# Seven half-block products for eight in the last batch's spatial gate of a fused attention and gated-MLP kernel

## Chip, cores and metric

The kernel runs on one core of a Trainium2 chip. Its time is the device time in microseconds of one execution; a number given for a kernel is the median of several runs. The profile is one further execution, taken by the hardware profiler, with a time of its own.

## What is computed

Four batches, 1088 positions, 128 model columns (4 heads of 32). Attention comes first, with a kernel feature map of 64 features, then a gated MLP with a spatial gate. The reference, cut to what matters:

```python
x = attn_out.transpose(0, 2, 1, 3).reshape(B, S, H * D)    # [4, 1088, 128]
h = gelu_tanh(x @ w_in)                                    # [4, 1088, 1024]
u, v = h[..., :512], h[..., 512:]
v_n = (v - mean(v)) / sqrt(var(v) + 1e-6) * g_ln           # over the 512 columns
v_s = einsum('ts,bsd->btd', w_sg, v_n) + b_sg[None, :, None]
out = x + (u * v_s) @ w_out
```

The change is in the einsum with `w_sg`, a 1088 x 1088 matrix, for the last batch. That product is most of TensorE's work.

## The kernel before

**Words.** TensorE multiplies in float32r. For accuracy each float32 operand is split in two words, a high one (the value cast to float32r) and a low one (the value less the high word), and three products are summed: high x high, high x low, low x high. A "word h" is a cast on ScalarE or in a transfer on POOL's queue, a "word l" a subtraction on VectorE.

**The spatial product.** The sum over s is cut in nine row blocks t of 128 (the last is half full: both words stand on its two halves, so it takes two matmuls for three). The output is [128 columns d, rows of W]: four d-blocks `db`, and the 1088 rows in three thirds `ci` of 362, 362 and 364. A unit (db, ci) takes one PSUM bank and 8 x 3 + 2 = 26 matmuls: `z_hi` with both words of V (`parts`) on `w_h[t]`, `z_lo` with V's high word on `w_l[t]`. W's words stay in SBUF for the whole run: `w_h`, one tile of nine row blocks, written by casting transfers, and `w_l`, eight tiles, subtracted in batch 0 (`w_lo`).

**Around it.** `v1` makes v = x @ w_in for a row block, `gelu` takes it out of PSUM, `bn` takes its statistics, `norm` works out the scale and shift for the first five and then for the last four row blocks, on VectorE, and `v3` applies them on ScalarE. `vh` and `vl` split V. `pu` and `ug` make u for a unit. After a unit `gt` (`scale`) takes z out of PSUM with `g_col` and the bias on VectorE, `gm` (`gate`) multiplies with u, `gh` and `gl` split the result, and `po` adds its product with w_out to an accumulator that is open over the four d-blocks. `o1`, `o2` add x, `st` stores. The very last unit (3, 2) of batch 3 is done in two halves with an unsplit product (`last`). Attention of a batch (`k1` to `xl`) runs beside the spatial product of the batch before it; POOL makes its low words `ql`.

**What sets the order.** Every step is registered with `at(name, function)`, and `Steps.run` issues them by `WHEN`, a list written out with one place for each step. Each engine and each queue then runs its own instructions in that order. Steps are named here as they are in the code, `z 3 0 1 4` for `("z", 3, 0, 1, 4)`: batch, d-block, third, row block. SP's queue takes the plain transfers, POOL's the casting ones. Buffers come from one pool by tag; a tile waits until the last reader of the buffer's tile before has finished. PSUM has eight banks, all under one tag.

In the order before, batch 3 takes the units one after the other. Lines of the profile: L840 and L849 are `z_hi` and `z_lo`, L864 to L866 `unit`, L910 to L913 `out`, L877 `scale`, L884 `gate`, L889 and L892 `g_h` and `g_l`, L827 and L832 `split_h` and `split_l`, L708 `w_lo`, L749 `gelu`, L289 the casting load of W, L514 `ql`, L917 to L926 the last unit.

Of the kernel before, what the change touches and what calls it, by code (L numbers as in the profile page):

```python
# [1123 lines left out]
```

## Time and profile before

| | us |
|---|---|
| Median of 3 runs (327.08 to 327.32) | 327.14 |
| The profiled execution, its own time | 327.86 |
| Its span, from the first to the last instruction | 325.8 |
| TensorE busy | 318.4 (98%), 2282 matmuls |
| VectorE busy | 251.6 (77%) |
| ScalarE busy | 158.8 (49%) |
| POOL busy | 22.8 (7%) |

Matmuls are pipelined: a record lasts 0.32 us though the next one starts after half of that, so that a busy TensorE isn't one at its peak. An engine's waits, and the distance from one start to the next, say more. The granted clock is given as a share of 2.4 GHz.

### The profile page before, as it was taken

Reading aid. Unit: us, or ns where it says so; the run is one execution under the profiler, and the core shown is the slowest. Engines: PE = TensorE matmul, PEld = TensorE weight load, DVE = VectorE, ACT = ScalarE, POOL = GpSimd, SP = SyncE. Lnnn points to the kernel's source line nnn. Section 1 sums busy time; section 2 is a strip of 40 time slices with the busy share of each in tenths; the row PEclk is TensorE's granted clock in tenths of the full one; section 3 lists DMA queues with packets and bytes.
Section 4 is the critical chain, followed back from the end, with each engine's and each line's share of the span. In section 5 each row is a group of like instructions: output and inputs, shape, how many; then the busy total and the mean of one; then the engine's idle time right before and its main releaser. Section 6 shows DMA issues by size and latency. Waiting matters only on the chain.

```text
span 325.8 us, 5961 instructions
## 1 busy us (share of the span) xinstructions
PE 318.4 (98%) x2282; PEld 304.7 (93%) x2282; DVE 251.6 (77%) x614; ACT 158.8 (49%) x347; POOL 22.8 (7%) x35
## 2 busy tenths in 40 slices
PE   7999999999999999999999999999999999999995
PEld 5777999899999999999999999999999999999993
DVE  5899999999998967597988967768998874443243
ACT  4579714646549734354629815244634954131210
POOL 0300000022200000202200000112200000000000
PEclk9999999999999999999999999999999999999999
DMA  7999934774000115832000012551000000000002
GB/s 218 370 423 348 404 137 131 175 180 118 2 0 0 48 49 138 194 96 57 2 0 24 2 68 47 109 94 45 2 1 2 24 35 11 0 2 0 0 2 68
DMA packets 14091, 29.55 MB, mean 91 GB/s; under 512 B 1744, under 2 KB 10224, under 8 KB 13680
## 3 DMA queue, kind: packets, MB, share of 16 engines
q1 hardware_dynamic: 13344, 23.87, 25.1%
q0 software_dynamic: 720, 5.31, 4.3%
q8 instruction: 18, 0.29, 0.4%
q14 instruction: 9, 0.07, 0.1%
HBM read 23.19 MB, written 2.65 MB: 79 GB/s over the span
## 4 chain that ended last, share of the span: by engine, by line
PE 82%; DVE 11%; ACT 3%; DMA 2%; issue 1%; SPq 1%; ACTq 0%; DVEq 0%
PE pz L840 38%; PE pz L849 17%; PE pu L864 3%; DVE w_l L708 2%; PE po L913 2%; PE pu L866 2%; PE po L911 2%; PE pu L865 2%; PE po L910 2%; PE pkv L420 2%; PE pv L736 2%; PE pv L735 2%; PE pv L744 2%; DMA vn<-in_q 2%; PE pk L388 1%
## 5 line engine op out<-in xcount | busy, mean ns | idle before, releaser
L840 PE MATMUL pz<-w_h,vl 128*128 128x362 f32 (+1 forms) x432 | 140.1, 325 | 0.4 <-DVE vl L832 0.4
L840 PE MATMUL pz<-w_h,vh 128*128 128x362 f32 (+1 forms) x432 | 140.1, 325 | 0.0
L849 PE MATMUL pz<-w_l,vh 128*128 128x362 f32 (+1 forms) x384 | 118.0, 324 | 0.0
L840 PEld LDWEIGHTS pz<-w_h,vl 128*128 128x128 f32 x432 | 81.1, 188 | 1.4 <-DVE vl L832 0.9
L840 PEld LDWEIGHTS pz<-w_h,vh 128*128 128x128 f32 x432 | 81.1, 188 | 1.0 <-ACT u L871 0.3
L849 PEld LDWEIGHTS pz<-w_l,vh 128*128 128x128 f32 x384 | 71.1, 188 | 0.1
L877 DVE SCALAR_TENSOR_TENSOR gt<-pz,vi,b_bc 128x362 f32<-128x362 f32 (+3 forms) x49 | 28.5, 584 | 38.6 <-PE pz L840 38.3
L889 ACT CAST gh<-gt 128x362 fp32r<-128x362 f32 (+1 forms) x47 | 23.0, 493 | 53.6 <-DVE gt L884 49.8
L871 ACT ACTIVATE u<-pu 128x362 f32<-128x362 f32 (+1 forms) x48 | 22.7, 472 | 24.6 <-PE pu L866 16.2
L892 DVE TENSOR_TENSOR gl<-gt,gh 128x362 fp32r<-128x362 f32 (+1 forms) x47 | 26.4, 563 | 9.8 <-ACT gh L889 9.7
L827 ACT CAST vh<-vn 128x128 fp32r<-128x128 f32 (+1 forms) x72 | 25.8, 403 | 13.8 <-PE pz L840 13.4
L832 DVE TENSOR_TENSOR vl<-vn,vh 128x128 fp32r<-128x128 f32 (+1 forms) x72 | 28.5, 419 | 2.0 <-ACT vh L827 1.8
L817 ACT ACTIVATE vn<-vn,nm,rs 128x512 f32<-128x512 f32 x36 | 28.2, 811 | 2.6 <-DVE nm L811 2.5
L884 DVE TENSOR_TENSOR gt<-gt,u 128x362 f32<-128x362 f32 (+3 forms) x49 | 25.9, 528 | 0.9
L749 ACT ACTIVATE vn<-pv 128x512 f32<-128x512 f32 x36 | 21.0, 597 | 8.6 <-PE pv L744 7.7
L765 DVE BATCH_NORM_STATS2 st<-vn 128x6 f32<-128x512 f32 x33 | 22.5, 683 | 2.9 <-ACT vn L749 2.4
L535 DVE RECIPROCAL den<-den 128x362 f32<-128x362 f32 (+1 forms) x9 | 21.8, 2417 | 2.9 <-ACT den L530 2.9
L514 POOL TENSOR_TENSOR qpl<-e_0a,qph 128x362 fp32r<-128x362 f32 x6 | 6.5, 1103 | 145.2 <-ACT qph L509 145.2
L864 PE MATMUL pu<-x_h,win_h 128*128 128x362 f32 (+1 forms) x48 | 16.2, 338 | 0.0
L866 PE MATMUL pu<-x_l,win_h 128*128 128x362 f32 (+1 forms) x48 | 15.7, 327 | 0.0
L865 PE MATMUL pu<-x_h,win_l 128*128 128x362 f32 (+1 forms) x48 | 15.6, 326 | 0.0
L913 PE MATMUL po<-gl,wout_h 128*128 128x362 f32 (+1 forms) x47 | 15.5, 329 | 0.0
(181 smaller groups left out, 429.1 us busy)
## 6 DMA issues: line engine op xcount, KB each, us to landing
w_f<-in_w SPq DMA_DIRECT2D x9, 576.0 KB
w_h<-in_w POOLq DMA_DIRECT2D x2, 1152.0 KB, 8.9
vi<-in_v SPq DMA_DIRECT2D x7, 288.0 KB
w_h<-in_w POOLq DMA_DIRECT2D x1, 1728.0 KB, 15.7
k<-in_k SPq DMA_DIRECT2D x3, 576.0 KB
out<-o SPq DMA_DIRECT2D x8, 181.0 KB
w_h<-in_w POOLq DMA_DIRECT2D x2, 576.0 KB, 8.3
e_2a<-ab SPq DMA_DIRECT2D x6, 182.0 KB
```

Source lines behind the costliest of these rows:

```text
L765: V.bn_stats(st, self.vn[:, t])
L817: A.activation(self.vn[:, t], self.vn[:, t], AF.Identity, bias=self.nm[:, t : t + 1], scale=self.rs[:, t : t + 1])
L827: A.copy(self.parts[db][0][:, ts], self.vn[:, ts, P * db : P * db + P])
L832: V.tensor_sub(vl[:, ts], self.vn[:, ts, P * db : P * db + P], f32(vh[:, ts]))
L840: mm(self.z[db, ci], lhsT=self.parts[db][i][:, t], rhs=T["w_h"][:, t, AT[ci] : AT[ci] + cw], start=(t == 0 and i == 0), stop=(t == NT - 1 ...
L849: mm(self.z[db, ci], lhsT=self.parts[db][0][:, t], rhs=T["w_l", t][:, AT[ci] : AT[ci] + CH[ci][1]], start=False, stop=False,)
L864: mm(pu, lhsT=T["win_h"][:, ws], rhs=xh[:, cs], start=True, stop=False)
L871: A.activation(self.u[db, ci], self.pu.pop((db, ci)), AF.Gelu_apprx_tanh)
L877: V.scalar_tensor_tensor(self.gt[db, ci][:, s], self.z[db, ci][:, s], T["g_col"][:, db : db + 1], T["b_bc"][:, c0 : c0 + cw][:, s], op0=AL ...
L884: V.tensor_mul(gt, gt, self.u[db, ci][:, s])
L889: A.copy(self.g[db, ci][0], self.gt[db, ci])
L892: V.tensor_sub(self.g[db, ci][1], self.gt.pop((db, ci)), f32(self.g[db, ci][0]))
```

## The change

In batch 3 only, for the first two thirds of the rows (`ci` 0 and 1, 362 each) and the row blocks 0 to 7, the spatial product is taken as a 2 x 2 block product. The d-blocks go in two pairs, (0, 2) and (1, 3). With A the V blocks (two d-blocks x two halves of four row blocks) and B the W blocks (two halves x two thirds), the four results need eight products A x B of 4 row blocks; the new code takes seven, in four accumulators `x`, `w`, `u` and `v`, with sums of blocks as operands:

- sums of V (`s1` to `s4`), on VectorE, written over halves of `vn` that are no longer read;
- sums of W (`t1` to `t4`), by a copy and an accumulating transfer each in DRAM, in batches 0 to 2, on POOL's queue; in batch 3 they are loaded into SBUF once plain (`ldT`, into one buffer under `kld`; `ldT1`, into `vx` and one tile) and once cast (`Th`, `Th1`), and VectorE makes the low words (`Tl`, `Tl1`). `t1` goes over W's blocks of the second third, the others into buffers that attention has finished with;
- results by `take`: a product that belongs to several results is taken out of PSUM by VectorE several times, into running sums (`acc`, in `vx`) with plus or minus `g_col`, and the last time into `gt`.

The ninth row block is added with its own words (`edge`, `rest`). The last third keeps its 26 matmuls (`third`), with the new words' tiles. Each `product` has 4 x 3 matmuls. From step `z 2 0 1 4` on, the whole order `WHEN` is new: in batch 2, too, units of several d-blocks are interleaved, and attention of batch 3, the loads of the sums and the matmuls that don't need them stand in other places. Ahead of that only the eight transfers in DRAM and one small multiplication are put in. The pads, some tile sizes, and the tag of one small tile (`wout_f`) change as well.

```diff
+PAIRS = ((0, 2), (1, 3))
...
+    class Fast(Gate):
...
+        def sums(self, j, n):
+            d1, d2 = PAIRS[j]
+            a11, a12, a21, a22 = (self.half(d, k) for d in (d1, d2) for k in range(2))
+            o, x, y = {
+                "s1": (a22, a21, a22), "s3": (a21, a21, a11), "s2": (a22, a11, a22), "s4": (a12, a12, a22),
+            }[n]
+            V.tensor_sub(o, x, y)
...
+        def product(self, j, o, left, right, t, first):
+            p = self.open((j, o))[:, : CH[0][1]]
+            w = self.words[j, left]
+            h, l = self.right(right, t)
+            mm(p, lhsT=w[:, 0, t], rhs=h, start=first, stop=False, **GO)
+            mm(p, lhsT=w[:, 0, t], rhs=l, start=False, stop=False, **GO)
+            mm(p, lhsT=w[:, 1, t], rhs=h, start=False, stop=t == 3, **GO)
...
+        def take(self, j, o, db, ci, first, final, g):
+            c0, cw = CH[ci]
+            z, add = self.open((j, o))[:, :cw], T["b_bc"][:, c0 : c0 + cw]
+            if not first:
+                add = self.acc[db, ci]
...
+            V.scalar_tensor_tensor(to, z, T[g][:, db : db + 1], add, op0=ALU.mult, op1=ALU.add)
...
+    class Sums:
...
+        PARTS = (
+            ("t2", 2, 1, "s", 0), ("t2", 3, 1, "s", 1), ("t3", 2, 1, "q", 2), ("t2", 0, 2, "e", 3),
+            ("t3", 3, 1, "ab", 5), ("t3", 0, 2, "e", 6), ("t4", 0, 1, "r", 8), ("t4", 1, 3, "x", 9),
+        )
...
+        def copy(self, n):
+            self.d[n] = dram.tile([P, 4, WP], F32, tag=n, name=f"w{n}", bufs=1)
+            of = {"t1": (0, 0), "t3": (0, 1)}
+            nc.gpsimd.dma_start(self.d[n], self.block(*of[n]) if n in of else self.d["t1" if n == "t2" else "t2"])
+
+        def add(self, n):
+            of = {"t1": (0, 1), "t2": (1, 1), "t3": (1, 1), "t4": (1, 0)}[n]
+            nc.gpsimd.dma_start(self.d[n], self.block(*of), accum_op=ALU.add)
...
+        def load(self, i):
+            n, t, k, tag, at = self.PARTS[i]
+            if at // 3 not in self.raw:
+                self.raw[at // 3] = new([P, 3, WP], "kld", f"wr{at // 3}")
+            load(self.of(i), self.d[n][:, t : t + k])
...
+        def high(self, i):
+            n, t, k, tag, at = self.PARTS[i]
+            self.w[i] = h, l = [new([P, k, WP], tag, f"w{n}_{t}{x}", F32R) for x in "hl"]
...
+            nc.gpsimd.dma_start(h, self.d[n][:, t : t + k])
+
+        def low(self, i):
+            h, l = self.w[i]
+            V.tensor_sub(l[:, :, : CH[0][1]], self.of(i)[:, :, : CH[0][1]], f32(h[:, :, : CH[0][1]]))
...
+            third(d1)
+            products("x", a11, (0, 0), True)
...
+            for db, ci in ((d1, 1), (d2, 0), (d2, 1)):
+                taken("x", db, ci, first=True, g_col="ng_col" if ci else "g_col")
+            products("x", a12, (1, 0), False)
+            rest("x", d1, 0)
...
+            taken("x", d1, 0, first=True, final=True)
...
+            products("w", "s1", "t1", True)
+            taken("w", d2, 1)
+            products("w", "s4", (1, 1), False)
+            rest("w", d1, 1)
+            taken("w", d1, 1)
...
+            products("u", "s2", "t2", True)
...
+            taken("u", d1, 1, final=True)
...
+            products("u", "s3", "t3", False)
+            taken("u", d2, 0, g_col="ng_col")
+            rest("u", d2, 1)
...
+            taken("u", d2, 1, final=True)
+            products("v", a22, "t4", True)
+            rest("v", d2, 0)
...
+            taken("v", d2, 0, final=True)
...
-        g = Gate(b)
+        g = (Fast if b == B - 1 else Gate)(b)
```

## Rows read from the trace of the kernel before

**Rows 1.** The page, busy time: us, share of the span, instructions.

```profile
PE 318.4 (98%) x2282; PEld 304.7 (93%) x2282; DVE 251.6 (77%) x614; ACT 158.8 (49%) x347; POOL 22.8 (7%) x35
```

**Rows 2.** Waits of PE, whole run: us in total, times, longest.

```profile
PE pn L597 <- DMA vn<-in_q: 1.3, 2, 0.9
...
PE pz L840 <- DVE vl L832: 0.4, 1, 0.4
```

**Rows 3.** Stretches: length, busy us of PE, PEld, DVE, ACT, POOL; clock, DMA share, GB/s.

```profile
80.00:110.00 30.00, 30.00 (x176) 28.83 (x175) 28.17 (x78) 20.93 (x44) 2.16 (x3) 1.00 0.04 13
230.00:260.00 30.00, 30.00 (x178) 29.07 (x177) 27.25 (x73) 17.15 (x35) 0.98 (x1) 1.00 0.02 8
190.00:230.00 40.00, 40.00 (x330) 39.14 (x329) 28.19 (x59) 15.94 (x35) 5.13 (x5) 1.00 0.33 70
260.00:319.20 59.20, 59.20 (x368) 59.20 (x367) 25.53 (x51) 16.71 (x39) 0.00 (x0) 1.00 0.02 7
```

**Rows 4.** Timeline of PE: start, us; first and last matmul of unit (1, 1), batch 3.

```profile
279.50 0.32 PE L840 MATMUL pz<-w_h,vh 128*128 128x362 f32 x1
...
283.50 0.32 PE L840 MATMUL pz<-w_h,vl 128*128 128x362 f32 x1
```

**Rows 5.** Groups by line and form, 195 to 326 us (the last: 20 to 50).

```profile
L877 DVE SCALAR_TENSOR_TENSOR gt<-pz,vi,b_bc 128x362 f32<-128x362 f32 x14 | 8.3, 594 | 16.1 <-PE pz L840 16.0
L892 DVE TENSOR_TENSOR gl<-gt,gh 128x362 fp32r<-128x362 f32 x14 | 8.1, 581 | 5.4 <-ACT gh L889 5.4
L832 DVE TENSOR_TENSOR vl<-vn,vh 128x384 fp32r<-128x384 f32 x15 | 7.6, 550 | 0.0
L884 DVE TENSOR_TENSOR gt<-gt,u 128x362 f32<-128x362 f32 x14 | 7.5, 535 | 0.4
...
L827 ACT CAST vh<-vn 128x384 fp32r<-128x384 f32 x15 | 6.8, 510 | 9.0 <-PE pz L840 9.0
...
L749 ACT ACTIVATE vn<-pv 128x512 f32<-128x512 f32 x9 | 5.4, 597 | 3.6 <-PE pv L744 3.2
...
L832 DVE TENSOR_TENSOR vl<-vn,vh 128x128 fp32r<-128x128 f32 x9 | 2.5, 288 | 0.9 <-ACT vh L827 0.9
...
L827 ACT CAST vh<-vn 128x128 fp32r<-128x128 f32 x9 | 2.4, 293 | 0.1
...
L708 DVE TENSOR_TENSOR w_l<-w_f,w_h 128x1104 fp32r<-128x1104 f32 x8 | 10.4, 1301 | 0.0
```

**Rows 6.** Timeline of DVE, back to back: start, us.

```profile
264.79 0.54 DVE L884 TENSOR_TENSOR gt<-gt,u 128x362 f32<-128x362 f32 x1
265.24 1.02 DVE L832 TENSOR_TENSOR vl<-vn,vh 128x384 fp32r<-128x384 f32 x2
```

**Rows 7.** Waits of DVE, 190 to 326 us: in total, times, longest.

```profile
DVE gt L877 <- PE pz L840: 32.6, 17, 3.8
...
DVE gl L892 <- ACT gh L889: 8.0, 14, 0.7
```

**Rows 8.** POOL: issues (mean ns); landings in the page (KB, us); three operations.

```profile
L289 POOL DMA_DIRECT2D w_h<-in_w x5 | 2.8, 583 | 0.0
...
w_h<-in_w POOLq DMA_DIRECT2D x2, 1152.0 KB, 8.9
...
w_h<-in_w POOLq DMA_DIRECT2D x1, 1728.0 KB, 15.7
...
86.29 1.91 POOL L514 TENSOR_TENSOR qpl<-e_2a,qph 128x364 fp32r<-128x364 f32 x2 [7.10 <-ACT qph L509]
...
212.81 1.24 POOL L514 TENSOR_TENSOR qpl<-e_0a,qph 128x362 fp32r<-128x362 f32 x1 [1.50 <-ACT qph L509]
220.61 0.97 POOL L514 TENSOR_TENSOR qpl<-e_1a,qph 128x362 fp32r<-128x362 f32 x1 [6.55 <-ACT qph L509]
```

**Rows 9.** The chain that ended last, in order of time, after the last `z`.

```profile
319.18 0.03 issue
...
322.07 0.27 DVE o L926
```

More of the change, by code (lines that the diff above doesn't have):

```diff
@@ L31 @@
 SUMS = (0,1,2)
+PAIRS = ((0, 2), (1, 3))
+GO = dict(skip_group_check=True)
 WARM = 14
@@ L280, in w_f @@
     def w_f(t):
+        if "pad_w" not in T:
+            const("pad_w", [P, 40])
         if ("w_f", t) not in T:
@@ L291, in gate_wh @@
     def gate_wh():
-        G.tensor_copy(new([P, 40], "wait", "wait", I32)[:, :1], T["vi"].bitcast(I32)[:, :1])
+        G.tensor_copy(new([P, 64], "wait", "wait", I32)[:, :1], T["vi"].bitcast(I32)[:, :1])
     def gate_wf():
@@ L447, in load_q @@
             c0, cw = CH[ci]
-            self.q[ci] = q = new([P, CW], "q", f"q{self.b}_{ci}")
+            self.q[ci] = q = new([P, WP], "q", f"q{self.b}_{ci}")
             load(q[:, :cw], qd[self.b, :, c0 : c0 + cw])
@@ L610, in qa @@
     def qa(c, p):
-        if "pad_r" not in T:
-            const("pad_r", [P, 32])
         a_s[c, p] = new([P, WP], "r", f"a0_{c}{p}")[:, :n0]
@@ L895, in prepare @@
             if i == 0:
-                self.wf = new([P, C], "kld", "wout_f")
+                self.wf = new([P, C], "kp", "wout_f")
                 V.tensor_add(self.wf, f32(T["wout_h"][:, NB - 1]), f32(T["wout_l"][:, NB - 1]))
@@ L934, in store, with __init__, half, block @@
             load(outd[self.b, :, c0 : c0 + cw][:, s], self.o[ci][:, s])
+    class Fast(Gate):
+        SLOT = dict(s1="vh", s2="vh", s3="vl", s4="vl")
+        def __init__(self, b):
+            super().__init__(b)
+            self.words, self.acc, self.bank, self.n = {}, {}, {}, {}
+        def half(self, db, k):
+            return self.vn[:, 4 * k : 4 * k + 4, P * db : P * db + P]
+        def block(self, j, n):
+            if (j, n) not in self.words:
+                tag = self.SLOT[n] if n in self.SLOT else "vl" if n[1] else "vh"
+                self.words[j, n] = new([P, 2, NT // 2, P], tag, f"wb{self.b}_{j}{n if n in self.SLOT else n[0] + 4 * n[1]}", F32R)
+            return self.words[j, n]
+        def edge(self, db):
+            if db not in self.words:
+                self.words[db] = new([P, 2, P], "kb", f"we{self.b}_{db}", F32R)
+            return self.words[db]
+        def source(self, j, n):
+            d1, d2 = PAIRS[j]
+            return self.half(*{"s1": (d2, 1), "s2": (d2, 1), "s3": (d2, 0), "s4": (d1, 1)}.get(n, n))
+        def word_h(self, j, n, t0, k):
+            A.copy(self.block(j, n)[:, 0, t0 : t0 + k], self.source(j, n)[:, t0 : t0 + k])
+        def word_l(self, j, n, t0, k):
+            w = self.block(j, n)
+            V.tensor_sub(w[:, 1, t0 : t0 + k], self.source(j, n)[:, t0 : t0 + k], f32(w[:, 0, t0 : t0 + k]))
+        def edge_h(self, db):
+            A.copy(self.edge(db)[:, 0], self.vn[:, NT - 1, P * db : P * db + P])
+        def edge_l(self, db):
+            w = self.edge(db)
+            V.tensor_sub(w[:, 1], self.vn[:, NT - 1, P * db : P * db + P], f32(w[:, 0]))
+        def sums(self, j, n):
+            d1, d2 = PAIRS[j]
+            a11, a12, a21, a22 = (self.half(d, k) for d in (d1, d2) for k in range(2))
[3 more added lines that the diff above has]
+            V.tensor_sub(o, x, y)
+        def right(self, n, t):
+            if n[0] == "t":
+                return T[n, t]
+            k, ci = n
+            cs = slice(AT[ci], AT[ci] + CH[ci][1])
+            return T["w_h"][:, 4 * k + t, cs], T["w_l", 4 * k + t][:, cs]
+        def open(self, o):
+            if o not in self.bank:
+                self.bank[o] = bank(f"pz{self.b}_{o}")
+            return self.bank[o]
+        def product(self, j, o, left, right, t, first):
[5 more added lines that the diff above has]
+            mm(p, lhsT=w[:, 1, t], rhs=h, start=False, stop=t == 3, **GO)
+        def rest(self, j, o, db, ci):
+            p = self.open((j, o))[:, : CH[0][1]]
+            for i in range(2):
+                mm(
+                    p, lhsT=self.words[db][:, i], rhs=T["w_h"][:, NT - 1, AT[ci] : AT[ci] + CH[ci][1]],
+                    start=False, stop=i == 1, **GO,
+                )
[4 more added lines that the diff above has]
+                add = self.acc[db, ci]
+            if final:
+                to = self.gt[db, ci] = new([P, CW], "gt", f"gt{self.b}_{db}_{ci}")[:, :cw]
+            elif first:
+                i = db // 2 if ci else 2
+                to = self.acc[db, ci] = T["vx"].rearrange("p n c -> p (n c)")[:, WP * i : WP * i + cw]
+            else:
+                to = add
+            V.scalar_tensor_tensor(to, z, T[g][:, db : db + 1], add, op0=ALU.mult, op1=ALU.add)
+        def third(self, db, t):
+            j, m = db % 2, db // 2
+            ci = len(CH) - 1
+            cs = slice(AT[ci], AT[ci] + CH[ci][1])
+            if t == 0:
+                self.z[db, ci] = bank(f"pz{self.b}_{db}_{ci}")[:, : CH[ci][1]]
+            if t == NT - 1:
+                for i in range(2):
+                    mm(self.z[db, ci], lhsT=self.words[db][:, i], rhs=T["w_h"][:, t, cs], start=False, stop=i == 1)
+                return
+            w = self.words[j, (db, t // 4)]
+            for q, (i, r) in enumerate(((0, T["w_h"][:, t]), (0, T["w_l", t]), (1, T["w_h"][:, t]))):
+                mm(self.z[db, ci], lhsT=w[:, i, t % 4], rhs=r[:, cs], start=(t == 0 and q == 0), stop=False)
+        def out(self, db, ci):
+            cw = CH[ci][1]
+            k = self.n[ci, "o"] = self.n.get((ci, "o"), 0) + 1
+            if k == 1:
+                self.po[ci] = bank(f"po{self.b}_{ci}")[:, :cw]
+            o = self.po[ci]
+            gh, gl = self.g.pop((db, ci))
+            mm(o, lhsT=T["wout_h"][:, db], rhs=gh, start=(k == 1), stop=False)
+            mm(o, lhsT=T["wout_l"][:, db], rhs=gh, start=False, stop=False)
+            mm(o, lhsT=T["wout_h"][:, db], rhs=gl, start=False, stop=k == NB - (ci == len(CH) - 1))
@@ new lines, in tile_kernel, with __init__, block, of @@
+    class Sums:
+        PARTS = (
+            ("t2", 2, 1, "s", 0), ("t2", 3, 1, "s", 1), ("t3", 2, 1, "q", 2), ("t2", 0, 2, "e", 3),
+            ("t3", 3, 1, "ab", 5), ("t3", 0, 2, "e", 6), ("t4", 0, 1, "r", 8), ("t4", 1, 3, "x", 9),
+        )
+        def __init__(self):
+            self.d, self.raw, self.w = {}, {}, {}
+        def block(self, k, ci):
+            return wd[:, 4 * k : 4 * k + 4, AT[ci] : AT[ci] + WP]
+        def copy(self, n):
[5 more added lines that the diff above has]
+            nc.gpsimd.dma_start(self.d[n], self.block(*of), accum_op=ALU.add)
+        def of(self, i):
+            n, t, k, tag, at = self.PARTS[i]
+            return self.raw[at // 3][:, at % 3 : at % 3 + k]
+        def load(self, i):
[4 more added lines that the diff above has]
+        def high(self, i):
+            n, t, k, tag, at = self.PARTS[i]
+            self.w[i] = h, l = [new([P, k, WP], tag, f"w{n}_{t}{x}", F32R) for x in "hl"]
+            for m in range(k):
+                T[n, t + m] = h[:, m, : CH[0][1]], l[:, m, : CH[0][1]]
+            nc.gpsimd.dma_start(h, self.d[n][:, t : t + k])
+        def low(self, i):
+            h, l = self.w[i]
+            V.tensor_sub(l[:, :, : CH[0][1]], self.of(i)[:, :, : CH[0][1]], f32(h[:, :, : CH[0][1]]))
+        def first(self, t):
+            v = T["vx"].rearrange("p n c -> p (n c)")[:, : 3 * WP].rearrange("p (n c) -> p n c", c=WP)
+            return v[:, t] if t < 3 else self.last
+        def load1(self, i):
+            if i:
+                self.last = new([P, WP], "wa", "wa")
+                load(self.last, self.d["t1"][:, 3])
+            else:
+                v = T["vx"].rearrange("p n c -> p (n c)")[:, : 3 * WP].rearrange("p (n c) -> p n c", c=WP)
+                load(v, self.d["t1"][:, :3])
+        def high1(self):
+            cs = slice(AT[1], AT[1] + CH[1][1])
+            for t in range(4):
+                T["t1", t] = T["w_h"][:, t, cs], T["w_l", t][:, cs]
+            nc.gpsimd.dma_start(T["w_h"][:, :4, cs], self.d["t1"][:, :, : CH[1][1]])
+        def low1(self, t):
+            h, l = T["t1", t]
+            V.tensor_sub(l, self.first(t)[:, : CH[1][1]], f32(h))
@@ L950, in gated @@
             return last(g, db, ci)
-        at(("gt", g.b, db, ci), lambda: g.scale(db, ci))
+        if not (isinstance(g, Fast) and ci < 2):
+            at(("gt", g.b, db, ci), lambda: g.scale(db, ci))
         at(("gm", g.b, db, ci), lambda: g.gate(db, ci))
@@ L1027, in main, with fast, pair, words @@
                 gated(g, db, ci)
+    def fast(g):
+        w = Sums()
+        at("ng", lambda: V.tensor_scalar_mul(const("ng_col", [P, NB]), T["g_col"], -1.0))
+        for n in ("t1", "t2", "t3", "t4"):
+            at(("wd", n), lambda n=n: w.copy(n))
+            at(("wd", n, 1), lambda n=n: w.add(n))
+        for i in range(len(w.PARTS)):
+            at(("ldT", i), lambda i=i: w.load(i))
+            at(("Th", i), lambda i=i: w.high(i))
+            at(("Tl", i), lambda i=i: w.low(i))
+        for i in range(2):
+            at(("ldT1", i), lambda i=i: w.load1(i))
+        at("Th1", w.high1)
+        for t in range(4):
+            at(("Tl1", t), lambda t=t: w.low1(t))
+        def pair(j, d1, d2):
+            def words(n, step):
+                for t in range(0, 4, step):
+                    at(("vh", g.b, j, n, t), lambda t=t: g.word_h(j, n, t, step))
+                    at(("vl", g.b, j, n, t), lambda t=t: g.word_l(j, n, t, step))
+            def products(o, left, right, first):
+                for t in range(4):
+                    at(("p", g.b, j, o, left, t), lambda t=t: g.product(j, o, left, right, t, first and t == 0))
+            def taken(o, db, ci, first=False, final=False, g_col="g_col"):
+                if final:
+                    at(("gt", g.b, db, ci), lambda: g.take(j, o, db, ci, first, True, g_col))
+                    gated(g, db, ci)
+                else:
+                    at(("tk", g.b, j, o, db, ci), lambda: g.take(j, o, db, ci, first, False, g_col))
+            def rest(o, db, ci):
+                at(("p8", g.b, j, o, db, ci), lambda: g.rest(j, o, db, ci))
+            def third(db):
+                unit(g, db, 2)
+                for t in range(NT):
+                    at(("z", g.b, db, 2, t), lambda t=t: g.third(db, t))
+                gated(g, db, 2)
+            a11, a12, a21, a22 = ((d, k) for d in (d1, d2) for k in range(2))
+            for n in (a11, a12):
+                words(n, 4 if j else 1)
+            at(("vh", g.b, j, 8, d1), lambda: g.edge_h(d1))
+            at(("vl", g.b, j, 8, d1), lambda: g.edge_l(d1))
+            third(d1)
+            products("x", a11, (0, 0), True)
+            for n in (a21, a22):
+                words(n, 4)
+            at(("vh", g.b, j, 8, d2), lambda: g.edge_h(d2))
+            at(("vl", g.b, j, 8, d2), lambda: g.edge_l(d2))
+            for db, ci in ((d1, 1), (d2, 0), (d2, 1)):
+                taken("x", db, ci, first=True, g_col="ng_col" if ci else "g_col")
+            products("x", a12, (1, 0), False)
+            rest("x", d1, 0)
+            unit(g, d1, 0)
+            taken("x", d1, 0, first=True, final=True)
+            if not j:
+                third(d2)
+            at(("s", g.b, j, "s1"), lambda: g.sums(j, "s1"))
+            words("s1", 4)
+            for n in ("s3", "s2", "s4"):
+                at(("s", g.b, j, n), lambda n=n: g.sums(j, n))
+            words("s4", 4)
+            products("w", "s1", "t1", True)
[3 more added lines that the diff above has]
+            taken("w", d1, 1)
+            words("s2", 4)
+            products("u", "s2", "t2", True)
+            unit(g, d1, 1)
+            taken("u", d1, 1, final=True)
+            words("s3", 4)
+            products("u", "s3", "t3", False)
+            taken("u", d2, 0, g_col="ng_col")
+            rest("u", d2, 1)
+            unit(g, d2, 1)
+            taken("u", d2, 1, final=True)
+            products("v", a22, "t4", True)
+            rest("v", d2, 0)
+            unit(g, d2, 0)
+            taken("v", d2, 0, final=True)
+            if j:
+                third(d2)
+        for j, (d1, d2) in enumerate(PAIRS):
+            pair(j, d1, d2)
@@ L1077, in tile_kernel @@
                 at(("prep", i), lambda i=i, g=g: g.prepare(i))
-        main(g, 0)
+        if b == B - 1:
+            fast(g)
+        else:
+            main(g, 0)
     steps.run(tc)
```

5 lines of the change are left out of this document (4 added, 1 removed), and 130 rows, old and new, of the table WHEN.

## The prediction

> **What bounds the kernel now.** I read the page's busy shares first, then the engine's waits, then the stretches, then single instructions. TensorE is busy 98% of the span [rows 1]; that alone doesn't make it the bound, since matmuls overlap in the records. The waits settle it: over the whole run PE's longest wait is 1.3 us, for a load at the start, and the one on VectorE's word `vl` is 0.4 us [rows 2]. Between 80 and 319 us there is no stretch in which PE is below its full length [rows 3]. So a matmul less in batch 3 shortens the run by the time from one matmul's start to the next, as long as nothing makes PE wait. That time isn't the recorded 0.32 us: in unit (1, 1) of batch 3 the first matmul starts at 279.50 and the 26th at 283.50, 25 steps in 4.00 us, 0.160 us each for 362 columns [rows 4]. The granted clock is 1.00 in every stretch [rows 3], the 2.4 GHz level.
>
> **What it removes.** For each pair of d-blocks, (0, 2) and (1, 3), and the first two thirds of the rows, eight half products of 4 x 3 matmuls become seven. The ninth row block (`rest`) and the last third (`third`) keep their counts: 84 + 4 x 2 + 2 x 26 = 144 matmuls a pair for 6 x 26 = 156. Two pairs save 24, all of 362 columns: 24 x 0.160 = **3.85 us** off PE [rows 4]. The Trainium skill ("TensorE: Matmul & The Clock Gate", section "Back-to-back issue gap") gives N/2.4 + 2.5 ns for a lone warm matmul, 153 ns for 362 columns; by it the same 24 would be worth an estimated 3.7 us.
>
> **What it adds to VectorE.** Durations are from [rows 5]. A 512-column word or sum is not in the trace; from 288 ns at 128 and 550 ns at 384 columns, 1.02 ns a column, it comes to 0.68 us as recorded. Words of V: before 9 x 0.29 + 9 x 0.55 = 7.6 us in batch 3, after 12 x 0.29 + 14 x 0.68 = 13.0, so +5.4. Sums of V: 8 x 0.68 = +5.4. Takes out of PSUM: 20 for 8 scales, 12 x 0.59 = +7.1. Low words of W's sums: 16 tiles of 362 columns in 12 instructions, nine at 0.55, two estimated at 0.93 and one at 1.30 (the price of 1104 columns): +8.1. Together **26 us** as recorded. Back to back they cost less, since the next one starts 0.45 us after one of 0.54, and two of 0.55 take 1.02 [rows 6]: some 23 to 24 us. Between 190 and 319.2 us VectorE is busy 28.2 + 27.3 + 25.5 = 81 us of 129 [rows 3], so on the mean there is room (105 of 125). ScalarE gets eight more high words and larger ones: 12 x 0.29 + 14 estimated at 0.62 against 9 x 0.29 + 9 x 0.51, +5 us on 50 busy [rows 3, 5]; I cost it at nothing, hidden by the 79 us that it is free; without that cover it is the 5 us.
>
> **Where it is tight.** The order is written out, so I counted it. From the last step of the first normalisation group of batch 3 (`norm 3 0 10`) to the low word of s3 of pair 0, VectorE has 76 instructions. With back-to-back prices (0.11 for a norm step, 0.22 for 128 columns, 0.47 for 362, 0.55 from PSUM, 0.62 for 512) they sum to 33.3 us. PE has 239 matmuls there, 38.5 us. VectorE may stand idle 5.2 us, 13% of the stage, before PE waits. The nearest stretch of before is 230 to 260, the same work (normalisation, scales, words): VectorE is idle 9% of it, and PE is not idle at all [rows 3]; at that share it is 3.5 us, which fits. In the stretch 80 to 110 VectorE is 94% busy and PE still full [rows 3]. Within the stage one handover is narrower: from the last matmul of `x` with a11 to the first with s1 PE has 42 matmuls, 6.7 us, and VectorE two takes in between, then the sum s1 and its words, 6.0 us without a wait. So I charge **0.8 us** of PE stalls, for two or three such handovers; the ends are 0 (as in 230 to 260) and 6.2 us (at the idle share of 190 to 230, 29% of 38.5 us is 11.4, less the 5.2) [rows 3]. I take a value near the lower end because the idle time of before is mostly VectorE waiting for PE's next result (`gt` on `pz`, 32.6 us in 17 waits [rows 7]), which comes from having little to do, and the new order gives it work there.
>
> **The order and the banks.** From `z 2 0 1 4` on, batch 2's units of up to three d-blocks are interleaved; their matmuls stay the same in number, so the move itself costs PE nothing. What it costs is banks, of which there are eight. The narrowest place that I found: `z 2 3 2` opens in the bank that `gelu 3 6` frees. Between `v1 3 6` and it PE has three matmuls of `v1 3 5` and nine of z, some 2.1 us; ScalarE has three GELUs of 0.60 [rows 5], 1.8 us. It fits by 0.3 us; were ScalarE a step behind it would be 0.3 us of stall, within the 0.8.
>
> **Transfers.** Four copies and four accumulations of 768 KB in DRAM, ten loads and nine cast loads of the sums, issued on POOL's and SP's queues. On POOL they stand among the `ql` subtractions, which PE needs for `q3`: an issue there took 0.58 us on the mean [rows 8]. Two copies stand ahead of `ql 1 5` and `ql 1 4`; POOL is idle 7.1 us before those now [rows 8], so I cost them at nothing; were that cover gone it would be 1.2 us. An accumulation reads twice what it writes and no row shows one. From the loads of W, 1152 KB in 8.9 us and 1728 KB in 15.7 us at a time when the DMA engines were full [rows 8], 768 KB is 6 to 7 us, and three streams of it 21 us at most; below, it may be 5 us. The first two have about 100 us before their words are read, the last some 35, and DMA share is 0.02 to 0.04 in 80 to 110 and 230 to 260 [rows 3]: hidden, cost nothing. The reloads of the one raw buffer (`kld`) are nearer: after `Tl 6` releases it, `ldT 7` (576 KB) must land before `Tl 7`, with about 7 us of VectorE work between. 576 KB at the price of the 1152 KB row is 4.5 us: hidden.
>
> **The end.** After the last matmul of the last `z`, before has 9 matmuls of `po` and a VectorE chain from 319.18 to 322.34 [rows 9]. The new order leaves 18 there (`pu 3 3 2` and five `po`), so that `z` ends 9 x 0.16 = 1.4 us earlier; but VectorE then has two gates and two low words more (about 0.5 each, some of it beside the wait for `ug 3 3 2`), an estimated 4.4 us of chain for 3.2. Net -0.2 us; bounds -1.4 and +0.8.
>
> **The sum.** -3.85 - 0.2 + 0.8 = -3.3 us. The profiled execution took 327.86 us (its span 325.8 and 2.1 around it), 0.7 above the median of the three runs; it would be 324.6 after, and the median 327.14 - 3.3 = 323.9.
>
> **Rivals.**
> 1. *VectorE becomes the bound between the batches (slower).* The place is the stage above. It decides the sign when VectorE's idle time there passes 5.2 + 4.05 = 9.2 us, 24% of 38.5: every microsecond more is one that PE stands. Against it: 9% in 230 to 260; for it: 29% in 190 to 230, where it waits for attention's results [rows 3], and the many new handovers from ScalarE (`gl` on `gh`, 8.0 us in 14 waits [rows 7]). At 29% the stall is 6.2 us and the time 327.14 - 4.05 + 6.2 = 329.3 us. Chance 0.10.
> 2. *The transfers are late.* The raw buffer is refilled three times, and the queue on POOL runs beside a busy VectorE. POOL's own operations already show it: the same subtraction took 0.97 us alone and 1.24 us at 212.81 [rows 8]. If a refill took 8.9 us, like the loads of W at the start, VectorE would stand 2 us at each, 6 us in all, more than the 5.2 that it has: with the 3.5 of other waits, 4.3 us of stall and 327.4 us. Against it: the DMA engines are nearly idle there [rows 3]. The Trainium skill ("SBUF - State Buffer", section "Who interferes with whom") says that a transfer issued from GpSimd waits for its descriptors while VectorE holds the shared ports, and that a two-input VectorE operation holds off GpSimd's reads; it would make this rival likelier. The 0.58 us issues at the start show no such wait, but no row has an issue inside the stage. Chance 0.06.
> 3. *The saving is given back in many small waits*, some 0.3 us at each of a dozen products, since a product needs both words and a free bank: 327.1 us, no change. PE's one 0.4 us wait on `vl` [rows 2] is the size. Chance 0.04.
>
> That the change doesn't remove what it says I exclude by the count above.
>
> **The numbers.** Forecast 0.80, all faster; its own range is 322.9 (no stall, the end at its better bound in part) to 326.4. Rival 1 is slower, rival 2 half and half, rival 3 no change: slower 0.13, same 0.07. A measurement of this kernel tells about 0.2%, 0.65 us, from no change. The range 322.9 to 326.9 leaves out rival 1, most of rival 2 and a little at the low end.
>
> **What would show it.** Right: 24 fewer PE instructions (2258); PE's waits after 190 us below 1.5 us, the longest on `words` or `take`; VectorE's busy time up by 23 to 26 us; the stage around 245 to 285 at over 85% VectorE with PE full; the first two thirds of the trace unchanged to 0.3 us. Wrong: PE slices below 9 around the batch change, with `vl` or `vh` as releaser (rival 1), or VectorE waiting for `wr` or for the cast words (rival 2), or POOL's `qpl` behind a transfer with PE waiting for `pnd`.

## The result and the profile after

The changed kernel took 323.96 us (median of 4 runs, 323.18 to 324.53); the kernel before, beside it, 327.13 (327.08 to 327.32). The ratio is 0.990, 95% interval 0.9876 to 0.9925. The forecast was 323.9, in a range of 322.9 to 326.9. The profiled execution took 323.18 us, its span 321.4. Beside the runs of the study, on two chips, the same two kernels gave ratios of 0.9876 and 0.9853 (below), so the saving is 1.0 to 1.5% of the time.

The page of the changed kernel: busy time of each engine, and landings (KB each, median us).

```profile
PE 314.4 (98%) x2258; PEld 300.7 (94%) x2258; DVE 273.2 (85%) x655; ACT 161.9 (50%) x355; POOL 35.1 (11%) x52
...
wt<-in_w POOLq DMA_DIRECT2D x6, 768.0 KB, 7.5
...
wt<-wt POOLq DMA_DIRECT2D x2, 768.0 KB, 6.7
...
wt_1h<-wt POOLq DMA_DIRECT2D x1, 576.0 KB, 4.6
```

PE has 24 instructions less than in [rows 1] and is 4.0 us less busy; VectorE is 21.6 us more busy, POOL 12.3, ScalarE 3.1. Six of the 768 KB transfers read W (two copies, four accumulations), two copy a sum made before.

The three longest of PE's six waits over the whole run (total, times, longest), the answer to [rows 2]:

```profile
PE warm L197 <- POOL vi L180: 0.9, 1, 0.9
PE pk L397 <- DMA k<-in_k: 0.7, 2, 0.5
PE pz L847 <- DVE vl L839: 0.4, 1, 0.4
...
```

All six lie before 190 us; none names a `wb`, a `wt` word or a `take`. A delay of up to 0.16 us hardly shows there, though, since the record before it (0.32 us, with 0.16 from start to start) still counts as busy. It shows as a wait of the weight load (PEld), which goes ahead of each matmul. From 190 to 318 us the two longest of four such waits are:

```profile
PEld pu L871 <- DVE gt L884: 0.3, 1, 0.3
PEld pz L847 <- DVE vl L839: 0.3, 1, 0.3
```

The other two, 0.2 us each at `pk` and `pkv`, are there before the change as well. The stretches of the changed kernel, with the columns of [rows 3]; the last is the stage that the prediction called tight, from the last step of the first normalisation group of batch 3 to the low word of s3:

```profile
80.00:110.00 30.00, 30.00 (x175) 28.83 (x174) 28.19 (x79) 20.95 (x44) 6.47 (x8) 1.00 0.66 148
190.00:230.00 40.00, 39.99 (x328) 38.61 (x327) 30.20 (x52) 15.35 (x34) 8.73 (x11) 1.00 0.53 134
230.00:260.00 30.00, 30.00 (x176) 28.90 (x175) 26.18 (x80) 18.12 (x37) 1.30 (x2) 1.00 0.21 60
260.00:290.00 30.00, 30.00 (x187) 30.00 (x186) 25.23 (x50) 11.02 (x26) 0.53 (x1) 1.00 0.25 77
290.00:315.00 25.00, 25.00 (x155) 24.94 (x154) 20.74 (x41) 7.54 (x17) 0.00 (x0) 1.00 0.01 2
...
246.60:284.12 37.52, 37.52 (x232) 37.52 (x231) 32.46 (x77) 20.04 (x44) 0.53 (x1) 1.00 0.21 63
```

Before, VectorE had little to do behind 260 us: 25.5 of 59.2 us [rows 3]. Now it is busy 83 to 87% from 230 to 315 us, and PE's row stays full beside it. In the stage VectorE stands idle 37.52 - 32.46 = 5.06 us, 13.5%; the prediction had 13%.

**Where the time went.** The start scatters from profile to profile: in the ten of this study the first `pk` matmul of batch 1 begins between 53.86 and 55.66 us after the span's start, in the three of the changed kernel alone between 53.88 and 55.58. So I also take the length from that matmul to the end of VectorE's last `o`, which leaves the scatter out. In the two kernels' timelines, before:

```profile
54.58 1.27 PE L388 MATMUL pk<-sk,k 128*64 128x64 f32 x36
...
322.00 0.35 DVE L926 TENSOR_TENSOR o<-pl,o 128x184 f32<-128x184 f32 x1
```

and after:

```profile
54.09 1.27 PE L397 MATMUL pk<-sk,k 128*64 128x64 f32 x36
...
317.97 0.33 DVE L933 TENSOR_TENSOR o<-pl,o 128x180 f32<-128x180 f32 x1
```

Before it is 322.35 - 54.58 = 267.77 us, after 318.30 - 54.09 = 264.21: 3.56 less. The same length in the profile of each run of the study:

| kernel | median us of its runs | first `pk` to last `o`, us |
|---|---|---|
| before | 327.13; beside e0 to e3 327.8, beside e4 to e7 327.76 | 267.77 |
| changed, the result | 323.96 | 264.21 |
| e0_again, changed | 323.72 | 263.66 |
| e7_after_beside, changed | 322.99 | 264.02 |
| e1_sums_in_dram_only | 327.71 | 267.88 |
| e2_24_matmuls_back | 327.48 | 267.83 |
| e3_no_sums_of_w | 323.31 | 263.99 |
| e4_low_words_of_w_twice | 323.53 | 264.60 |
| e5_low_words_of_v_twice | 327.43 | 268.04 |
| e6_both_twice | 335.08 | 275.09 |

The three profiles of the changed kernel give 263.96 on the mean, 3.81 less than before.

The medians hold one thing more that this length leaves out. A run's time less its span is 2.02 us on the mean for the kernel before and 1.78 for the changed one. It is 1.76 in e1 too, which only adds the transfers in DRAM, and 2.07 in e3, which has none of them; why isn't shown. So up to 0.3 us of a difference of medians lies outside the span.

### The profile page after: what moved, and what is told of

Its sections match the earlier page's. It is cut to its first block, busy times and chain, and to the rows that moved or that the text cites. A ratio compares the mean times of both kernels' runs of the same rounds, so it can differ in the third digit from the quotient of the medians.

```text
span 321.4 us, 6043 instructions
## 1 busy us (share of the span) xinstructions
PE 314.4 (98%) x2258; PEld 300.7 (94%) x2258; DVE 273.2 (85%) x655; ACT 161.9 (50%) x355; POOL 35.1 (11%) x52
## 4 chain that ended last, share of the span: by engine, by line
PE 91%; DVE 6%; DMA 1%; ACT 1%; issue 0%; SPq 0%; DVEq 0%; ACTq 0%
PE pz L847 33%; PE pz L856 14%; PE pz L1046 5%; PE pkv L429 3%; PE pu L871 3%; PE pu L872 2%; PE pu L873 2%; PE pv L743 2%; PE pv L742 2%; PE pv L751 2%; PE po L920 2%; PE po L918 2%; PE po L917 2%; PE pk L397 1%; DMA k<-in_k 1%; DVE vn L205 1%
## 5 line engine op out<-in xcount | busy, mean ns | idle before, releaser
L847 PE MATMUL pz<-w_h,vl 128*128 128x362 f32 (+1 forms) x324 | 105.3, 325 | 0.4 <-DVE vl L839 0.4
L847 PE MATMUL pz<-w_h,vh 128*128 128x362 f32 (+1 forms) x324 | 105.5, 326 | 0.0
L856 PE MATMUL pz<-w_l,vh 128*128 128x362 f32 (+1 forms) x288 | 87.0, 324 | 0.0
L847 PEld LDWEIGHTS pz<-w_h,vl 128*128 128x128 f32 x324 | 60.8, 188 | 1.9 <-DVE vl L839 1.2
L847 PEld LDWEIGHTS pz<-w_h,vh 128*128 128x128 f32 x324 | 60.8, 188 | 1.3 <-ACT u L878 0.3
L856 PEld LDWEIGHTS pz<-w_l,vh 128*128 128x128 f32 x288 | 53.1, 188 | 0.1
L884 DVE SCALAR_TENSOR_TENSOR gt<-pz,vi,b_bc 128x362 f32<-128x362 f32 (+3 forms) x41 | 23.5, 578 | 6.8 <-PE pz L847 6.1
L756 ACT ACTIVATE vn<-pv 128x512 f32<-128x512 f32 x36 | 21.0, 597 | 11.9 <-PE pv L751 11.1
L839 DVE TENSOR_TENSOR vl<-vn,vh 128x128 fp32r<-128x128 f32 (+1 forms) x54 | 22.4, 432 | 1.2 <-ACT vh L834 0.9
L834 ACT CAST vh<-vn 128x128 fp32r<-128x128 f32 (+1 forms) x54 | 19.5, 403 | 5.7 <-PE pz L847 5.3
L1046 PE MATMUL pz<-w_h,wb 128*128 128x364 f32 x64 | 18.8, 324 | 0.0
```

What stands on the lines that cost most here:

```text
L839: V.tensor_sub(vl[:, ts], self.vn[:, ts, P * db : P * db + P], f32(vh[:, ts]))
L847: mm(self.z[db, ci], lhsT=self.parts[db][i][:, t], rhs=T["w_h"][:, t, AT[ci] : AT[ci] + cw], start=(t == 0 and i == 0), stop=(t == NT - 1 ...
L856: mm(self.z[db, ci], lhsT=self.parts[db][0][:, t], rhs=T["w_l", t][:, AT[ci] : AT[ci] + CH[ci][1]], start=False, stop=False,)
L884: V.scalar_tensor_tensor(self.gt[db, ci][:, s], self.z[db, ci][:, s], T["g_col"][:, db : db + 1], T["b_bc"][:, c0 : c0 + cw][:, s], op0=AL ...
L1046: mm(self.z[db, ci], lhsT=w[:, i, t % 4], rhs=r[:, cs], start=(t == 0 and q == 0), stop=False)
```

## The experiments

Theory P is the prediction's: PE is the bound, a matmul less is 0.160 us less, and VectorE and the transfers have room. Theory V: VectorE has become, or nearly become, the bound. Theory T: the transfers cost time. Runs e0 to e3 shared one chip and one set of runs of the kernel before (median 327.8), e4 to e7 another chip and another set (327.76).

**e0_again** is the changed kernel without an edit.

> The changed kernel once more, to see its spread (its four runs lie between 323.18 and 324.53) and a second profile. Theory P (TensorE is the bound, 24 matmuls of 0.160 us are gone): median 323.2 to 324.5, ratio 0.988 to 0.992; in a profile of a slower run the extra time stands ahead of 80 us or as PE waits in batch 3. Theory V (VectorE has become the bound around the change of batches, by a little that differs from run to run): PE waits of 0.5 to 1.3 us between 245 and 290 us, released by VectorE or ScalarE. Theory T (transfers that land late): PE or VectorE waiting for a transfer of the sums.

323.72 us (322.6 to 325.33, 6 runs), ratio 0.9876 [0.9848, 0.9904]. The difference is there again, 4.1 us between the medians, a little more saved than theory P's ratio of 0.988 to 0.992. The profile, of a run at 324.11, has its extra time ahead of 80 us, as P said: its first `pk` is at 55.58 us, for 54.09.

**e1_sums_in_dram_only**: the kernel before, with the four copies and four accumulations added at the places where the changed kernel issues them. Nothing reads the sums.

```diff
+    w = Sums()
+    at(("wd", "t1"), lambda: w.copy("t1"))
+    at(("wd", "t1", 1), lambda: w.add("t1"))
...
```

> The kernel before, with nothing but the four copies and four accumulating transfers in DRAM put in at their places on POOL's queue; nothing reads the sums. Theory P: no change, 327.1 +- 0.3, since POOL and the DMA engines are idle there. Theory T: slower by 0.3 to 1.5 us, by the low words ql behind an issue (0.6 to 1.2 us each at two places) or by loads that wait; then the saving of the matmuls is larger than 3.2 us and part of it is paid here.

327.71 us (326.95 to 328.52, 12 runs), ratio 0.9998 [0.9985, 1.0012]; the length is 267.88 against 267.77. (Theory P's 327.1 was the kernel before in the first runs; beside this one it is at 327.8.) The transfers did run: between 80 and 110 us the DMA engines' share is 0.65, for 0.04 in [rows 3], and PE is full, in the stretches of this run:

```profile
80.00:110.00 30.00, 30.00 (x176) 28.83 (x174) 28.16 (x78) 20.96 (x44) 6.45 (x8) 1.00 0.65 147
```

So sums of W's blocks that are made in DRAM cost nothing here, under 0.4 us by the interval.

**e2_24_matmuls_back**: the changed kernel, but each pair's product of s1 with t1 is issued twice, so that PE has the 24 matmuls back that the change removes. The doubled product makes the output another one.

```diff
-            mm(p, lhsT=w[:, 0, t], rhs=h, start=first, stop=False, **GO)
...
+            for i in range(2 if left == "s1" else 1):
+                mm(p, lhsT=w[:, 0, t], rhs=h, start=first and i == 0, stop=False, **GO)
...
```

> The changed kernel with the product of s1 and t1 done twice in both pairs, 24 matmuls of 362 columns more (V's product with this sum enters twice, so the result differs there). Theory P: +3.85 us against the changed kernel, 327.4 to 328.2, with 2282 matmuls as before. Theory V: less than 2.5 us, since the matmuls put back fill time in which PE waits for VectorE.

327.48 us (326.58 to 328.36, 10 runs), 3.76 above e0_again beside it; the length is 3.87 above the mean of the three changed ones, and within 0.06 of the kernel before. 24 x 0.160 is 3.85 [rows 4]. So by the length the whole gain is those 24 matmuls. Everything else that the change does, the new order, VectorE, ScalarE, POOL and the queues, comes to nothing together. That is a balance and not the absence of costs: the next part finds 0.57 us won at the end and 0.60 on the mean lost before it. By the times this run's ratio to the kernel before is 0.9975 [0.9958, 0.9993], 0.2 to 1.4 us faster, of which 0.26 us lies outside the span (1.76 for 2.02).

**e3_no_sums_of_w**: the changed kernel without the sums of W: no transfer for them, no reload, no low word. The products that want a sum read a plain block of W, so the output is another one.

```diff
-            at(("Tl", i), lambda i=i: w.low(i))
+            at(("Tl", i), lambda: None)
...
-            k, ci = n
+            k, ci = {"t1": (0, 1), "t2": (1, 1), "t3": (0, 0), "t4": (1, 0)}.get(n, n)
```

> The changed kernel without the sums of W: no copies and accumulations in DRAM, no loads and cast loads of the sums, none of VectorE's twelve low words (8 us of its work); the products take the plain blocks of W in their place, so the output leaves the sums out. The order and the matmuls stay. Theory P: the same as the changed kernel within 0.5 us. Theory V or T: faster than the changed kernel by 0.8 us or more, V with VectorE's load around 245 to 290 us, T with the spread of the runs falling to that of the kernel before (0.2 us).

323.31 us (322.88 to 324.61, 6 runs), 0.41 under e0_again; the length is 263.99, the changed kernel's own. VectorE is 7.4 us less busy than in the page of after, and 12.5 of 42.1 MB of the traffic are gone, for nothing. Between them, this and e1 leave theory T no more than some 0.4 us. For theory V it says only that VectorE is not the limit now, not how near it is. The next three load VectorE in steps.

**e4_low_words_of_w_twice**: two subtractions for each low word of W's sums.

```diff
+            for _ in range(2):
-            V.tensor_sub(l[:, :, : CH[0][1]], self.of(i)[:, :, : CH[0][1]], f32(h[:, :, : CH[0][1]]))
+                V.tensor_sub(l[:, :, : CH[0][1]], self.of(i)[:, :, : CH[0][1]], f32(h[:, :, : CH[0][1]]))
...
```

> Each low word of the sums of W's blocks is subtracted twice; the second writes the same values. 5.3 us of VectorE work back to back are added in the stage from the first normalisation group's last step (norm 3 0 10) to the low word of s3, where the changed kernel's VectorE is idle 5.1 of 37.5 us and PE is never idle; another 2 us lie before it. Theory P (idle time of VectorE can be filled; PE stands only for what doesn't fit): the changed kernel beside it plus 0 to 1.2 us, PE waits in the stage 0.2 to 1.2 us. Theory V (VectorE idles because it waits for PE's products, so that time can't be filled, and added work is added time): plus 3.5 to 5.3 us.

323.53 us (322.6 to 323.81, 4 runs), 0.54 above e7_after_beside; the length is 0.64 above the mean. The stage, in the stretches of this run:

```profile
246.83:285.44 38.61, 38.60 (x237) 38.24 (x236) 38.16 (x86) 20.18 (x44) 0.53 (x1) 1.00 0.21 61
```

VectorE is busy 38.16 of 38.61 us and PE full. The stage is 1.1 us longer than in the changed kernel, since the low word of s3 comes that much later, and all but 0.45 us of VectorE's idle time is filled: it waited for PE's results because it was early, not because the work had to be so late. Theory V's "added work is added time" falls for the first 5 us. PE's waits from 190 us on are none, where theory P expected 0.2 to 1.2 us in the stage. The one new wait between 230 and 318 us stands under the weight loads, at 284.9 us, where a product first needs a low word of t4:

```profile
PEld pz_(0, 'v')_3674 L1009 <- DVE wt_1l L1104: 0.3, 1, 0.3
```

**e5_low_words_of_v_twice**: two subtractions for each low word of V's blocks and sums (`word_l`), the edit as in e4.

> Each low word of V's blocks and of their sums in batch 3 is subtracted twice, with the same values. 7.2 us of VectorE work are added in the stage and 4.2 us behind it. Theory P: 7.2 less 5.1 us of idle time, so plus 2.1 us, up to 3.5 if words come late one by one. Theory V: plus 5.5 to 7.2 us from the stage, and more behind it.

327.43 us (326.47 to 328.85, 10 runs), ratio to before 0.9994 [0.9979, 1.0010]: 4.4 above e7 (4.1 by the length) and the whole gain lost. That is in neither theory's range. Its stretches:

```profile
260.00:290.00 30.00, 28.59 (x172) 27.60 (x171) 29.51 (x58) 9.03 (x21) 0.53 (x1) 1.00 0.25 78
290.00:315.00 25.00, 24.33 (x143) 22.79 (x142) 23.31 (x44) 7.72 (x16) 0.00 (x0) 1.00 0.00 1
```

and PE's waits from 190 us on:

```profile
PE pz L1047 <- DVE wb L976: 0.8, 2, 0.6
PE pz_(0, 'u')_3615 L1011 <- DVE wb_0s L976: 0.6, 1, 0.6
PE po L1058 <- DVE gl L899: 0.3, 1, 0.3
PE pz_(0, 'w')_3535 L1011 <- DVE wb_0s L976: 0.3, 1, 0.3
```

Up to 290 us PE starts 15 matmuls less than in the changed kernel's row for 260 to 290, 2.4 us, near theory P's 7.2 less 5.1. Between 290 and 315 it starts another 12 less, 1.9 us. That part both theories had missed or left open: 4.2 us of words are added there too, and there PE waits for single words although VectorE still has 1.7 us of idle time.

**e6_both_twice**: both edits.

> Both kinds of low words are subtracted twice. 12.5 us of VectorE work are added in the stage. Theory P: 12.5 less 5.1, plus 7.4 us, up to 8.9; that is 3.5 to 5 us slower than the kernel before, the rival in which VectorE becomes the bound. Theory V: plus 9.5 to 12.5 us. If VectorE isn't the limit at all in that stage (work is done well ahead of its reader): under plus 4 us.

335.08 us (333.82 to 336.55, 4 runs), ratio to before 1.0223 [1.0186, 1.0260]; 12.1 above e7, 11.1 by the length. That is rival 1, the slower side. It is more than the 7.4 to 8.9 of theory P and within the 9.5 to 12.5 of theory V, whose reason, that VectorE's idle time can't be filled, e4 has shown false for the first 5 us. The trace shows where P's sum fell short. PE's waits between 255 and 300 us:

```profile
PE pz L1047 <- DVE wb L976: 2.7, 3, 1.5
PE pz_(0, 'u')_3626 L1011 <- DVE wb_0s L976: 2.0, 1, 2.0
PE po L920 <- DVE gl L899: 0.7, 1, 0.7
PE pz_(0, 'w')_3545 L1011 <- DVE wb_0s L976: 0.3, 1, 0.3
```

The waits are 5.7 us, half of the loss. They cost more than they show. In PE's timeline (start, us) the longest one stands between the first two of these lines, and the last two bound a stretch of 11 slow matmuls:

```profile
282.74 0.32 PE L1010 MATMUL pz_(0, 'u')_3626<-wt_0l,wb_0s 128*128 128x362 f32 x1
285.10 0.43 PE L1011 MATMUL pz_(0, 'u')_3626<-wt_0h,wb_0s 128*128 128x362 f32 x1 [2.03 <-DVE wb_0s L976]
285.37 0.33 PE L1009 MATMUL pz_(0, 'w')_3545<-w_h,wb_0s 128*128 128x362 f32 x1
...
286.45 0.51 PE L1009 MATMUL pz_(1, 'x')_3590<-w_h,wb 128*128 128x362 f32 x1
...
289.72 0.33 PE L1011 MATMUL pz_(0, 'u')_3626<-wt_2h,wb_0s 128*128 128x362 f32 x1
```

From 282.74 to 285.37 it is 2.63 us for two steps that otherwise take 0.32: 2.31 lost for 2.03 recorded. The six waits listed are 0.26 to 0.28 us dearer than their records each, 1.6 us together. The 11 steps from 286.45 to 289.72 take 3.27 us, where at 0.160 they take 1.76: another 1.5 us. The stretches show the granted clock beside them:

```profile
262.80:266.80 4.00, 1.84 (x10) 1.25 (x10) 3.93 (x9) 2.03 (x7) 0.00 (x0) 1.00 0.47 147
282.00:286.00 4.00, 1.97 (x12) 1.68 (x11) 3.93 (x8) 0.87 (x2) 0.00 (x0) 1.00 0.47 144
286.00:288.00 2.00, 2.00 (x10) 2.00 (x9) 1.94 (x5) 0.35 (x1) 0.00 (x0) 0.56 0.04 14
288.00:290.00 2.00, 2.00 (x9) 2.00 (x8) 1.67 (x4) 0.66 (x2) 0.00 (x0) 0.59 0.23 79
```

After the wait of 2.03 us the clock is 0.56 and 0.59 for 4 us, mostly the 1.2 GHz level. Between 262.80 and 266.80 PE stood for longer, in two waits, and the clock stayed at 1.00 up to 286 us; what decides it isn't shown. Waits, their surplus and the clock are 8.8 of the 11.1 us. The other 2.3 are not split up; behind 290 us the words of the second pair are late again, as in e5.

**e7_after_beside** is the changed kernel again, beside e4 to e6.

> The changed kernel, unchanged, on the same chip as the three others, which are compared with it. All theories: 3.2 to 4.1 us under the kernel before.

322.99 us (322.79 to 323.25, 4 runs), ratio 0.9853 [0.9838, 0.9868], 4.8 under the kernel before: 0.7 more than any theory said. The length, 3.75 under before's, doesn't show that 0.7; what is left for it are the starts, which scatter by 1.8 us, and 0.2 us outside the span (1.83 for 2.02).

The steps together: 5.3 us more in the stage cost 0.5; 7.2 us there and 4.2 behind it cost 4.4; both kinds of words cost 12.1. That fits an edge of VectorE's room where the prediction's count had put it, just above 5 us; no run lies between 5.3 and 7.2.

## Why the prediction was right, point by point

**The sum.** The range held and the largest term was right. That 323.96 stands 0.1 us from the forecast is luck: of the sum -3.85 - 0.2 + 0.8, the last two came to -0.57 and, on the mean of three profiles, +0.60, so that the length fell by 3.81 and not by 3.3. The three pairs of medians differ by 3.17, 4.08 and 4.77 us; the last is more than the range allowed, counted from the kernel before.

**The 24 matmuls.** Right: -3.85 was forecast, e2 gives 3.76 by medians and 3.87 by the length. For 24 matmuls the rule of the Trainium skill ("TensorE: Matmul & The Clock Gate", section "Back-to-back issue gap") came to an estimated 3.7; the trace's own step of 0.160 us [rows 4] is 4% above its 0.153, and the sum rightly went by the trace. The runs' times are too coarse to choose between 3.7 and 3.85.

**VectorE's 26 us.** The single prices held: a 512-column word or sum is 0.69 (0.68 estimated), the low words 0.91 (0.93) and 1.29 (1.30). The groups by form of the changed kernel, 190 to 322 us:

```profile
L990 DVE TENSOR_TENSOR vn<-vn 128x512 f32<-128x512 f32 x8 | 5.5, 686 | 0.1
...
L975 DVE TENSOR_TENSOR wb<-vn,wb 128x512 fp32r<-128x512 f32 x6 | 4.1, 690 | 0.6 <-ACT wb L971 0.4
...
L1103 DVE TENSOR_TENSOR wt_0l<-wr,wt_0h 128x724 fp32r<-128x724 f32 x2 | 1.8, 905 | 0.0
...
L1103 DVE TENSOR_TENSOR wt_1l<-wr,wt_1h 128x1086 fp32r<-128x1086 f32 x1 | 1.3, 1293 | 0.0
```

The check on the page's busy time (+23 to 26) missed: it rose by 21.6. The busy time counts the overlap of two neighbours once, so the figure to set against it was the back-to-back sum of 23 to 24, and that was still 1.4 or more too high. ScalarE rose by 3.1 us for the 5 counted, and from 190 us on no wait of PE names it. The time didn't hang on it.

**The stage.** Right. 33.3 us of work in 38.5 was the count, 32.46 in 37.52 the measurement, and PE lost nothing there: its waits and those of its weight loads show none in the stage. One thing was too careful: the prediction took 3.5 of VectorE's 5.2 idle microseconds as waits that can't be filled. e4 filled all but 0.45. So rival 1 was further off than the prediction's own reading had it: with 5.3 us of unforeseen work in the stage the kernel was still faster, with 7.2 there and 4.2 behind it even, and e6 shows the rival itself at 335.08.

**The 0.8 us of stalls.** The size was right, the place wasn't. Up to the last `z` PE should have come 24 + 9 matmuls earlier, 33 x 0.160 = 5.28 us. From the first `pk`, the last `z` ends at 319.18 - 54.58 = 264.60 us before and at 314.26 - 54.09 = 260.17 after, 4.43 less: 0.85 lost. e0_again (315.19 - 55.58) and e7_after_beside (313.85 - 53.88) lose 0.29 and 0.65. They aren't handovers in the stage. From the first `pk` of batch 1 to that of batch 2, where little but POOL's queue differs, it is 67.88 us after and 67.85 before. Most of the loss in the profiled run of the result is in the two waits of weight loads shown above, in the interleaved end of batch 2: at 209.85 us `pu` waits for VectorE's `gt`, which frees a bank, and at 224.92 a `z` waits for VectorE's low word `vl`; each costs some 0.3 us. In e7_after_beside the first alone is there, in e0_again neither. So the mechanism, PE standing for a bank or a word at a few handovers, was the one that the prediction named, and it struck in another place: for late banks there it had looked at `z 2 3 2` only.

**The end.** A gain, as forecast, and larger: -0.57 for -0.2. The changed kernel's chain that ended last, behind the last `z`:

```profile
313.93 0.33 PE pz L1042 x2
314.26 0.16 PE pu L871
...
315.56 0.17 PE po L1057
...
315.82 0.98 DVE gl L899 x2
316.79 0.26 DVE o L933
317.05 1.00 DVE o L930 x2
```

From the end of `z` to the last `o` it is 318.30 - 314.26 = 4.04 us, for 4.4 estimated and 3.17 before [rows 9]; with 1.44 for the nine matmuls moved behind it, 4.04 - 3.17 - 1.44 = -0.57. The gates run beside the nine `po`, and of the two further d-blocks only the low words `gl` stand in the chain.

**The transfers.** Right that they cost nothing (e1, e3). An accumulation was bounded by 21 us and supposed at 5 or more; the four land 7.3 to 9.2 us after their issue. An issue was priced at 0.58 us; an accumulation's holds POOL for twice that, 1.16 to 1.20. POOL's timeline of the changed kernel shows what its queue stood behind (start, us; idle before):

```profile
78.68 1.52 POOL L1078 DMA_DIRECT2D wt<-in_w  x2
85.84 1.91 POOL L523 TENSOR_TENSOR qpl<-e_2a,qph 128x364 fp32r<-128x364 f32 x2 [5.64 <-issue]
87.69 1.20 POOL L1082 DMA_DIRECT2D wt<-in_w  x1
96.48 1.17 POOL L1082 DMA_DIRECT2D wt<-in_w  x1 [7.59 <-DMA wt<-in_w]
97.12 1.08 POOL L1078 DMA_DIRECT2D wt<-wt  x1
106.48 1.19 POOL L1082 DMA_DIRECT2D wt<-in_w  x1 [8.29 <-DMA wt<-wt]
```

The copies are issued in the idle time ahead of `qpl`, which still begins at 85.84 (86.29 in [rows 8]). The waits of 7.59 and 8.29 us for a transfer to land block the queue when nothing that PE needs stands in it. The prediction hadn't priced these waits; its cover, POOL's idle time, took them.

**Rival 2** rested on a rule of the Trainium skill ("SBUF — State Buffer", section "Who interferes with whom"), by which a transfer issued from GpSimd gets no descriptors while VectorE holds the ports that the two share. In the stage VectorE was busy 87% of the time and the one issue there took 0.53 us (0.58 before, [rows 8]); the 576 KB landed in 4.6 us, for 4.5 expected of that size; VectorE waited for no load of W's sums. So nothing was late. No run here shows the rule at work; with one issue in the stage they don't refute it either.

**Rival 3** is excluded by its size: 0.3 to 0.85 us lost, not a dozen times 0.3. (A dozen times 0.3 would have made it 327.14 - 4.05 + 3.6 = 326.7 us, not 327.1.) The bank place, `z 2 3 2` behind `gelu 3 6`, made no wait of PE.

## What to carry to other kernels

When one engine is full from end to end, price a saved instruction by the step from start to start, then ask only whether the engine that takes over the work has room in the tightest stage, with back-to-back prices counted along its order. That count is good for finding an edge: here it said 5.2 us, added work of 5.3 us was nearly free, and beyond it the loss grew faster than the count alone says: 4.1 us by the length for 7.2 us of work there and 4.2 behind it. To see delays of a few tenths, look at the waits of the weight loads too; a full row of matmuls hides them. To find what a change is worth part by part, put the saved work back alone (e2) and take the added work out alone (e3).
